# Attention and mixture-of-experts kernel on one core: a decay table made by running products, and another order of loads and transposes at the first expert

## Chip, cores and metric

One Trainium2 chip, one of its cores. The metric is device microseconds of one execution; the kernel before has a median of 269.46 us over three runs (268.55 to 269.71). Engines are TensorE (PE; its weight loads are PEld), VectorE (DVE), ScalarE (ACT), GpSimd (POOL) and SyncE (SP), each with its own queue of instructions, in order.

## The reference

Batch 2, 8 heads, 768 positions, head size 64. Attention is linear with a decay `lam[h]` per head, done in blocks; the result, 1536 tokens of 512, goes to 8 experts, one per token.

```python
intra = einsum('bhic,bhjc->bhij', qb, kb) * Dmask        # Dmask[i,j] = lam**(i-j) for i >= j, else 0
out   = einsum('bhij,bhjd->bhid', intra, vb) + einsum('bhid,bhde->bhie', qb * lam_pow, kv_state)
kv_state = lam_block * kv_state + einsum('bhsd,bhse->bhde', kb * rev_pow, vb)
...
expert = argmax(x @ w_gate); h = relu(x[expert] @ w1); y = gate * (h @ w2)     # w1 512x1024, w2 1024x512
```

## The kernel before, in words

**Attention** (`attention`, L245) works on 12 tiles of 128 tokens, one after the other (loop at L621). A tile needs two loads of 512 KB on SP's queue: `load(s, 0)` brings q and k ("qk"), `load(s, 1)` brings k and v ("kv"); four of each are in flight. `score(s)` (L413, PE at L427) makes the products q k, `mask(s)` (L431, DVE at L437) multiplies them by the decay table `dt`, `decay_k(s)` and `decay_q(s)` (POOL, L406 and L395) scale k by `kp` and q by `qp`, `state(s)` (PE L486, DVE L494 or L496) adds k v to the running state, `attend(s)` (PE L453, L460, ACT L465) makes the output, and `turn`, `gate`, `place`, `scatter` transpose it, choose the expert and write the rows into a DRAM buffer `xs`, sorted by expert. Scores run two tiles ahead; everything of a tile on one engine stands in the written order.

**The decay tables** are made ahead of the loop (L265 to L324). `lam_sb` is loaded; DVE doubles powers of lambda into `z8` on 8 partitions (L279 to L284, one row a head: 127 zeros, a one, then powers); PE transposes a piece of it for `kp` (L302, L303); `z8` is written to the DRAM table `zd` (L305) and read back twice as `dt`, each partition at its own offset (L309). In SP's queue the write stands behind `load(0, 1)` and ahead of `load(1, 0)`; the two reads stand ahead of `load(1, 1)` and of all loads of tiles 2 and 3. DVE then doubles powers into `qp` (L317 to L324). `busy(n)` (L287) issues n matmuls on constants, whose result nothing reads. Between `decay_k(0)` and `decay_q(1)` POOL issues four small DMAs of the gate weights `wg` into `iw` (L606). `tokens()` (L373) is seven small POOL operations on token numbers.

**The experts.** Weights come in pieces of 512 KB, 8 per expert, numbered through (piece 8 is the first of expert 1), in a ring of four raw buffers: `load_w(i)` (L97) on SP, `split_hi(i)` (L104) on ACT rounds it, `split_lo(i)` (L112) on DVE takes the rest and frees the raw buffer. Expert 0 is run in two halves of 128 rows, `first` and `second`, objects of `Solo` (L182): `turn` transposes the rows on PE, `up` is one quarter of the first matrix (12 matmuls of 256 columns, after each second one an ACT evacuation at L216), `cross` transposes the hidden values back (PE L221, ACT L223, DVE L224), `down` is a quarter of the second matrix (6 matmuls of 512 columns). `first` begins within attention; `second` is in `ffn` (L745 to L788). `load_rows(e)` (L138) reads an expert's rows from `xs` and must wait for `pad(e, 0)` and `pad(e, 1)` (POOL, indirect writes that clear unused rows, L129). For experts 1 to 7 (loop at L794, 256 rows at once) the rows are transposed on DVE by `shuffle(e, g)` (L719; the first call also makes the token numbers, L170) and split into two parts by `trans(e, g)` (ACT L729, DVE L730), two of four slices of columns each. The matmuls at L806 of expert 1 read the result, slice by slice.

What sets the order is the text itself: it is compiled with a manual schedule, so each engine runs its instructions in the order written, and each waits for what it reads or overwrites.

Of the kernel before, what the change touches and what calls it, by code (L numbers as in the profile page):

```python
# [41 lines left out]
def kernel(  # L42
# [29 lines left out]
    zd = dram.tile([H, 256], F32, name="zd")  # L72
# [42 lines left out]
    def split_w(i):  # L115
        split_hi(i)
        split_lo(i)
# [127 lines left out]
    def attention():  # L245
        with ExitStack() as c2:
# [10 lines left out]
            def load(s, half):  # L257

                if s >= NTILE:
                    return  # L260
                ld[s, half] = ld_p.tile([P, 2 * DM], F32, tag=f"ld{half}", name="qk" if half == 0 else "kv")
                c = slice(2 * DM * half, 2 * DM * half + 2 * DM)
                nc.sync.dma_start(out=ld[s, half], in_=qkv[s // NC, s % NC, :, c])

            lam_sb = ac.tile([P, HP + 1], F32, name="lam_sb")  # L265
            nc.sync.dma_start(out=lam_sb, in_=lam)
# [3 lines left out]
            z8 = p2.tile([P, 256], F32, tag="tmp", name="z8", bufs=1)[0:H]  # L270
            qp = ac.tile([P, HP, P], F32, name="qp")
            warm = ac.tile([P, 3 * P], F16, name="warm")
            make_identity(nc, ident)
            nc.vector.memset(warm, 1.0)
            one = ac.tile([P, 1], F32, name="one")
            nc.scalar.activation(out=one, in_=warm[:, 0:1], func=AF.Exp)
            nc.vector.memset(z8[:, 0:127], 0.0)
            nc.vector.memset(z8[:, 127:128], 1.0)
            nc.vector.tensor_copy(z8[:, 128:129], lam_sb[0:H, HP:HP + 1])  # L279
            n = 1  # L280
            while n < P:
                nc.vector.tensor_scalar(  # L282
                    out=z8[:, 128 + n:min(128 + 2 * n, 256)], in0=z8[:, 128:128 + n],
                    scalar1=z8[:, 127 + n:128 + n], scalar2=None, op0=ALU.mult,  # L284
                )
                n *= 2
# [9 lines left out]
            kp = ac.tile([P, H, 1], F32, name="kp")  # L296
# [3 lines left out]
            kps = lgb[:, 0:H]  # L300
            busy(11)
            nc.tensor.transpose(kps, z8[:, 127:255], ident[0:H, 0:H])  # L302
            nc.scalar.activation(out=kp, in_=kps, func=AF.Copy)  # L303
            busy(4)
            nc.sync.dma_start(out=zd, in_=z8)  # L305
            load(1, 0)
            dt = ac.tile([P, 2, HP, P], F32, name="dt")
            for t in range(2):
                nc.sync.dma_start(  # L309
                    out=dt[:, t],  # L310
                    in_=bass.AP(tensor=zd.tensor, offset=zd.offset + 256 * t, ap=[[1, P], [512, HP], [1, P]]),
                )
            load(1, 1)
            for i in range(2, 4):
                load(i, 0)
                load(i, 1)
            nc.vector.tensor_copy(qp[:, :, 0:1], lam_sb[:, 0:HP, None])  # L317
            n = 1
            while n < P:
                nc.vector.tensor_tensor(  # L320
                    out=qp[:, :, n:2 * n], in0=qp[:, :, 0:n],
                    in1=qp[:, :, n - 1:n].to_broadcast([P, HP, n]), op=ALU.mult,
                )
                n *= 2  # L324
# [279 lines left out]
            for g in range(2):  # L604
                for r in range(2):
                    nc.gpsimd.dma_start(  # L606
                        out=iw[64 * g:64 * g + 64, r::2, P:P + E], in_=wg[64 * r:64 * r + 64, 2 * g:2 * g + 2]
                    )
            decay_q(1)
            for a in range(HP):  # L610
                score(0, a)
            state(0, (0, 1, 2, 3))
            load(4, 0)
# [3 lines left out]
            busy(5, True)  # L617
            tokens()
            mask(0)
# [55 lines left out]
            load_rows(0, 1)  # L675
            pad(1, 0)
            pad(1, 1)
            load_rows(1)
            load_w(10)
# [3 lines left out]
            load_w(11)  # L683
            first.cross(0)
# [11 lines left out]
    def ffn(first):  # L696
        with ExitStack() as c2:
# [62 lines left out]
            split_hi(10)  # L760
            second.up(0)
            split_lo(10)
            load_w(14)
            second.up(1)
# [291 lines left out]
```

## Time and profile before

| | |
|---|---|
| median of 3 runs | 269.46 us (268.55 to 269.71) |
| profiled execution | 267.77 us, of which the span of the core's instructions 266.0 us |
| PE busy | 243.9 us (92%) |
| DVE, ACT, POOL busy | 157.3, 133.3, 82.5 us |
| mean granted PE clock | 0.967 of 2.4 GHz |
| DMA | 58.67 MB, 221 GB/s on the mean |

The profiled execution lies 1.7 us under the median. Busy PE time counts a matmul from its start to its end, and neighbours overlap; where PE is busy without a gap it sets the pace.

### The profile page before, as it was taken

To read this page: it belongs to the slowest core of one execution; us is meant where nothing else is said; L and a number is where in the kernel's file an instruction comes from. 1 tells how busy PE (TensorE), PEld (TensorE's weight loads), DVE (VectorE), ACT (ScalarE), POOL (GpSimd) and SP (SyncE) were. 2 spreads that over 40 slices of the span, in tenths; PEclk is the share of its full clock that TensorE was granted. 3 is DMA by queue.
4 is the path that set the end of the run, shared out by engine and by line. 5 is a ranking of instruction groups with operands and counts; after the bars stand their busy time and mean duration, and the time that the engine had idled before them with its cause. 6 is when DMAs were issued, how large, how long until landed. Compare 5 with 4: busy or idle time off the path is not lost.

```text
span 266.0 us, 5415 instructions
## 1 busy us (share of the span) xinstructions
PE 243.9 (92%) x2072; PEld 216.4 (81%) x2072; DVE 157.3 (59%) x336; ACT 133.3 (50%) x240; POOL 82.5 (31%) x102
## 2 busy tenths in 40 slices
PE   7679999998899697999999999999999999999960
PEld 3468888877798686988998998998898899899850
DVE  6234576988865267686479268478556937922100
ACT  2023547676674446665466466556545746622110
POOL 4943547998575301001400500410230020020030
PEclk9957999999999889999999999999999999999996
DMA  6997689995756963977498769869839798310010
GB/s 183 247 387 299 201 243 391 391 390 156 223 207 162 356 231 108 268 280 255 166 286 248 265 145 323 249 159 296 262 146 277 265 276 222 117 71 2 1 60 3
DMA packets 27390, 58.67 MB, mean 221 GB/s; under 512 B 5841, under 2 KB 14043, under 8 KB 27360
## 3 DMA queue, kind: packets, MB, share of 16 engines
q1 hardware_dynamic: 23696, 50.89, 60.3%
q0 software_dynamic: 3664, 7.38, 7.4%
q8 instruction: 18, 0.29, 0.5%
q14 instruction: 12, 0.10, 0.1%
HBM read 50.89 MB, written 11.57 MB: 235 GB/s over the span
## 4 chain that ended last, share of the span: by engine, by line
issue 58%; POOL 13%; PE 10%; DMA 8%; DVE 5%; ACT 2%; SPq 1%; POOLq 1%; DVEq 0%
POOL xs L129 6%; POOL out L176 4%; DMA qk<-in_qkv 3%; DMA wraw<-in_wp 3%; PE x L453 2%; PE sc L427 2%; PE tp L509 2%; DVE wlo L112 2%; PE st L486 1%; PE x L460 1%; DMA zd<-z 1%; POOL kd L406 1%; POOL out L869 1%; DMA lam_sb<-in_lam 1%; DVE z L282 1%
## 5 line engine op out<-in xcount | busy, mean ns | idle before, releaser
L112 DVE TENSOR_TENSOR wlo<-wraw,whi 128x1024 fp32r<-128x1024 f32 x64 | 77.3, 1216 | 16.6 <-ACT whi L104 16.6
L104 ACT ACTIVATE whi<-wraw 128x1024 fp32r<-128x1024 f32 x64 | 66.5, 1051 | 10.1 <-DMA wraw<-in_wp 10.1
L806 PE MATMUL h<-xh,whi 128*128 128x256 f32 x224 | 62.2, 278 | 1.5 <-ACT xh L729 1.5
L806 PE MATMUL h<-xl,whi 128*128 128x256 f32 x224 | 62.1, 277 | 0.3 <-DVE xl L730 0.3
L806 PE MATMUL h<-xh,wlo 128*128 128x256 f32 x224 | 62.0, 277 | 0.0
L176 POOL DMA_INDIRECT out<-y,ti x13 | 12.6, 973 | 124.6 <-ACT y L839 124.6
L814 DVE SCALAR_TENSOR_TENSOR hl<-h,hh 128x512 fp32r<-128x512 f32 x28 | 19.4, 692 | 42.2 <-ACT hh L813 42.2
L806 PEld LDWEIGHTS h<-xh,whi 128*128 128x128 f32 x224 | 42.0, 188 | 2.0 <-ACT xh L729 1.7
L806 PEld LDWEIGHTS h<-xl,whi 128*128 128x128 f32 x224 | 42.2, 188 | 0.8 <-DVE xl L730 0.5
L806 PEld LDWEIGHTS h<-xh,wlo 128*128 128x128 f32 x224 | 42.1, 188 | 0.0
L831 PE MATMUL y<-whi,hl 128*128 128x512 f32 x104 | 41.0, 394 | 0.0
L831 PE MATMUL y<-wlo,hh 128*128 128x512 f32 x104 | 40.9, 393 | 0.0
L831 PE MATMUL y<-whi,hh 128*128 128x512 f32 x104 | 40.5, 390 | 0.0
L813 ACT ACTIVATE hh<-h 128x512 fp32r<-128x512 f32 x28 | 16.8, 598 | 40.9 <-PE h L806 40.9
L831 PEld LDWEIGHTS y<-wlo,hh 128*128 128x128 f32 x104 | 19.5, 188 | 4.3
L831 PEld LDWEIGHTS y<-whi,hh 128*128 128x128 f32 x104 | 19.5, 188 | 4.1
L831 PEld LDWEIGHTS y<-whi,hl 128*128 128x128 f32 x104 | 19.6, 188 | 4.0
L437 DVE TENSOR_TENSOR pt<-sc,dt 128x512 f32<-128x512 f32 (+1 forms) x26 | 15.6, 643 | 7.5 <-PE sc L427 4.2
L465 ACT ACTIVATE xT<-x 128x512 f32<-128x512 f32 x12 | 7.1, 593 | 25.5 <-PE x L460 15.6
L129 POOL DMA_INDIRECT xs<-zero,padi x16 | 18.1, 1132 | 4.9 <-issue 4.3
L453 PE MATMUL x<-pt,kv 128*64 128x128 f32 x192 | 15.4, 300 | 1.9 <-DVE pt L437 1.9
L597 POOL DMA_INDIRECT xs<-xg,slot x12 | 16.0, 1333 | 3.7 <-ACT ex L543 1.2
(137 smaller groups left out, 361.2 us busy)
## 6 DMA issues: line engine op xcount, KB each, us to landing
wraw<-in_wp SPq DMA_DIRECT2D x64, 512.0 KB, 4.8
qk<-in_qkv SPq DMA_DIRECT2D x12, 512.0 KB, 7.8
kv<-in_qkv SPq DMA_DIRECT2D x12, 512.0 KB, 8.0
rw<-xs SPq DMA_DIRECT2D x28, 128.0 KB, 3.0
rw<-xs SPq DMA_DIRECT2D x2, 257.0 KB, 2.8
dt<-zd SPq DMA_DIRECT2D x2, 256.0 KB, 4.6
xs<-zero,padi POOLq DMA_INDIRECT x16, 3.5
out<-y,ti POOLq DMA_INDIRECT x13, 5.0
```

The lines of the kernel that those rows point to most:

```text
L104: nc.scalar.activation(out=hi, in_=raw[i], func=AF.Copy)
L112: nc.vector.tensor_tensor(out=lo, in0=t, in1=hi.bitcast(F32), op=ALU.subtract)
L129: i = nc.gpsimd.indirect_dma_start(out=xs, out_offset=bass.IndirectOffsetOnAxis(ap=padi[:, e, t:t + 1], axis=0), in_=zero, in_offset=None, ...
L176: i = nc.gpsimd.indirect_dma_start(out=out, out_offset=bass.IndirectOffsetOnAxis(ap=ti[e][:, t:t + 1], axis=0), in_=y, in_offset=None, bou ...
L437: nc.vector.tensor_tensor(out=pt[s][:, r, a], in0=sc[s][r][:, a], in1=dt[:, r, a], op=ALU.mult)
L453: nc.tensor.matmul(part(h), lhsT=v[:, h], rhs=pt[s][:, h % 2, h // 2], start=(h % 4 < 2), stop=True, skip_group_check=True,)
L465: nc.scalar.activation(out=xT[s], in_=x[:, :, 0:2 * P], func=AF.Copy)
L597: i = nc.gpsimd.indirect_dma_start(out=xs, out_offset=bass.IndirectOffsetOnAxis(ap=slot[:, s:s + 1], axis=0), in_=xg_all[:, s], in_offset= ...
L806: nc.tensor.matmul(ps[:, f], lhsT=a[:, k, fs], rhs=b[:, k], start=(n == 0), stop=(n == 3 * KD - 1),)
L813: nc.scalar.activation(out=hh, in_=ps, func=AF.Relu)
L814: nc.vector.scalar_tensor_tensor(out=hl, in0=ps, scalar=0.0, in1=hh.bitcast(F32), op0=ALU.max, op1=ALU.subtract)
L831: nc.tensor.matmul(yp[t], lhsT=a[:, f, tsl], rhs=b[:, f], start=(p == 0 and f == 0 and n == 0), stop=(p == 3 and f == 1 and n == 2),)
```

## The change

Three groups of edits. **(1) The tables.** `zd` and `z8` are gone. Lambda is loaded spread over all partitions (`lamb`); POOL makes `meet`, a matrix with ones on one antidiagonal; eight DVE scans along rows of 128 (multiply by lambda, add `meet`) write `dt` directly; `kp` is copied from its last column on ACT; `qp` is doubled to 32 columns ahead of `mask(0)` and to 128 behind it. All loads of tiles 1 to 3 are asked for at once, and the gate weights on ACT's queue at the start. `busy` goes from 11 and 4 to 14 early, and from 5 to 6 late. `mask(0)` moves ahead of `state(0)`, `decay_q(1)` behind the rest of `qp`, the gate weights' four DMAs away from POOL. **(2)** `load_w(10)` and `load_w(11)` stand ahead of `load_rows(1)`. **(3)** In `second`, both `shuffle(1, ...)` stand behind `up(0)`, `trans(1, 0)` behind `up(3)`, `trans(1, 1)` behind `down(1)`, and the splits of pieces 10 to 13 come later than they did.

```diff
-            lam_sb = ac.tile([P, HP + 1], F32, name="lam_sb")
-            nc.sync.dma_start(out=lam_sb, in_=lam)
+            lamb = ac.tile([P, 2, HP], F32, name="lamb")
+            nc.sync.dma_start(
+                out=lamb,
+                in_=bass.AP(tensor=lam.tensor, offset=lam.offset, ap=[[0, P], [D * (HP + 1), 2], [1, HP]]),
+            )
             load(0, 0)
             load(0, 1)
...
+            for g in range(2):
+                for r in range(2):
+                    nc.scalar.dma_start(
+                        out=iw[64 * g:64 * g + 64, r::2, P:P + E], in_=wg[64 * r:64 * r + 64, 2 * g:2 * g + 2]
+                    )
+            for i in range(1, 4):
+                load(i, 0)
+                load(i, 1)
...
+            nc.gpsimd.memset(meet, 0.0)
+            nc.gpsimd.affine_select(
+                out=meet, in_=meet, pattern=[[1, P]], compare_op=ALU.not_equal, fill=1.0,
+                base=1 - P, channel_multiplier=1,
+            )
...
-            nc.vector.tensor_copy(z8[:, 128:129], lam_sb[0:H, HP:HP + 1])
-            n = 1
-            while n < P:
-                nc.vector.tensor_scalar(
...
+            dt = ac.tile([P, 2, HP, P], F32, name="dt")
+            for a in range(HP):
+                for r in range(2):
+                    nc.vector.tensor_tensor_scan(
+                        out=dt[:, r, a], data0=lamb[:, r, a:a + 1].to_broadcast([P, P]), data1=meet,
+                        initial=0.0, op0=ALU.mult, op1=ALU.add,
+                    )
+
+            kp = ac.tile([P, H, 1], F32, name="kp")
+            nc.scalar.activation(
+                out=kp.rearrange("p (a r) o -> p a r o", r=2),
+                in_=dt[:, :, :, P - 1:P].rearrange("p r a o -> p a r o"), func=AF.Copy,
+            )
...
-            busy(11)
-            nc.tensor.transpose(kps, z8[:, 127:255], ident[0:H, 0:H])
-            nc.scalar.activation(out=kp, in_=kps, func=AF.Copy)
-            busy(4)
-            nc.sync.dma_start(out=zd, in_=z8)
-            load(1, 0)
-            dt = ac.tile([P, 2, HP, P], F32, name="dt")
-            for t in range(2):
-                nc.sync.dma_start(
...
+            busy(14)
+            def powers(n, end):
...
+            powers(1, 32)
...
             decay_k(0)
-            for g in range(2):
...
-            decay_q(1)
             for a in range(HP):
                 score(0, a)
+            load(4, 0)
+            mask(0)
+            busy(6, True)
+            powers(32, P)
+            decay_q(1)
             state(0, (0, 1, 2, 3))
-            load(4, 0)
             for a in range(HP):
                 score(1, a)
             load(5, 0)
-            busy(5, True)
             tokens()
-            mask(0)
             mask(1)
...
             load_rows(0, 1)
+            load_w(10)
             pad(1, 0)
             pad(1, 1)
-            load_rows(1)
-            load_w(10)
             first.up(2)
             split_hi(7)
             split_lo(7)
             load_w(11)
+            load_rows(1)
...
             second.rest()
-            split_hi(10)
             second.up(0)
-            split_lo(10)
-            load_w(14)
+            shuffle(1, 0)
+            shuffle(1, 1)
             second.up(1)
-            split_hi(11)
+            split_w(10)
+            load_w(14)
             second.up(2)
             second.cross(0)
-            split_lo(11)
+            split_w(11)
             load_w(15)
             second.up(3)
+            trans(1, 0)
+            second.down(0)
+            second.cross(1)
             split_w(12)
             load_w(16)
-            second.down(0)
-            second.cross(1)
-            shuffle(1, 0)
             second.down(1)
-            trans(1, 0)
+            trans(1, 1)
             split_w(13)
             load_w(17)
-            shuffle(1, 1)
             second.down(2)
-            trans(1, 1)
```

## Rows read from the trace of the kernel before

**Rows 1.** The page, part 1: busy us, share of the span, instructions.

```profile
PE 243.9 (92%) x2072; PEld 216.4 (81%) x2072; DVE 157.3 (59%) x336; ACT 133.3 (50%) x240; POOL 82.5 (31%) x102
```

**Rows 2.** Busy time by stretch: PE, PEld, DVE, ACT, POOL; then PE clock, DMA share, GB/s.

```profile
90.00:92.00 2.00, 1.01 (x6) 1.01 (x7) 1.23 (x1) 1.66 (x3) 0.00 (x0) 0.82 1.00 401
92.00:94.00 2.00, 2.00 (x12) 2.00 (x10) 1.16 (x2) 0.81 (x2) 0.00 (x0) 0.50 0.95 340
94.00:98.00 4.00, 4.00 (x20) 3.32 (x20) 2.64 (x5) 2.15 (x3) 0.00 (x0) 0.91 0.56 191
...
125.00:147.00 22.00, 22.00 (x146) 19.99 (x145) 14.71 (x17) 12.75 (x16) 3.94 (x5) 1.00 0.80 239
```

**Rows 3.** Timeline of PE, 84 to 106 us: start, us, instruction, [idle before, releaser].

```profile
84.65 0.28 PE L211 MATMUL solo_ps<-whi,solo_xh 128*128 128x256 f32 x1
...
86.01 0.28 PE L211 MATMUL solo_ps<-whi,solo_xh 128*128 128x256 f32 x1
...
90.99 0.87 PE L221 MATMUL solo_ps<-ident,solo_raw 128*128 128x128 f32 x4 [2.10 <-ACT solo_raw L216]
...
102.75 0.38 PE L806 MATMUL h<-xh,whi 128*128 128x256 f32 x1 [1.47 <-ACT xh L729]
103.48 0.38 PE L806 MATMUL h<-xl,whi 128*128 128x256 f32 x1 [0.34 <-DVE xl L730]
```

**Rows 4.** Timeline of ACT, 73 to 112 us.

```profile
89.39 1.06 ACT L104 ACTIVATE whi<-wraw 128x1024 fp32r<-128x1024 f32 x1 [3.85 <-DMA wraw<-in_wp]
90.36 0.58 ACT L216 ACTIVATE solo_raw<-solo_ps 128x512 f32<-128x512 f32 x1
```

**Rows 5.** Timeline of DVE, 73 to 112 us.

```profile
97.84 0.71 DVE L719 STREAM_TRANSPOSE xf<-rw 128x512 f32<-128x512 f32 x1
...
101.33 0.70 DVE L719 STREAM_TRANSPOSE xf<-rw 128x512 f32<-128x512 f32 x1
```

**Rows 6.** Timeline of SP's queue, 73 to 112 us (a merged row holds waits between its issues).

```profile
79.76 0.33 SPq L162 DMA_DIRECT2D rw<-xs  x1
81.80 1.82 SPq L146 DMA_DIRECT2D rw<-xs  x4
...
84.22 22.57 SPq L97 DMA_DIRECT2D wraw<-in_wp  x10
```

**Rows 7.** The tile rw: time from issue to landing of the loads of rows.

```profile
DMA to landing us min/median/max: 2.4/2.9/7.9
```

**Rows 8.** Timeline of all engines, 0 to 26 us: what the first tiles wait for.

```profile
2.65 1.76 DVE L282 TENSOR_SCALAR z<-z 8x1 f32<-8x1 f32 x7
...
4.51 1.85 DVE L320 TENSOR_TENSOR qp<-qp 128x4 f32<-128x4 f32 x7
...
8.16 0.43 SPq L263 DMA_DIRECT2D qk<-in_qkv  x1
...
10.42 1.31 POOL L395 TENSOR_TENSOR qd<-qk,qp 128x512 f32<-128x512 f32 x1
10.49 0.42 DVE L437 TENSOR_TENSOR pt<-sc,dt 128x256 f32<-128x256 f32 x1 [1.44 <-DMA dt<-zd]
...
13.03 0.21 POOL L380 TENSOR_SCALAR xg<-tokf 128x12 f32<-128x12 f32 x1
14.87 1.04 POOL L406 TENSOR_TENSOR kd<-kv,kp 128x512 f32<-128x512 f32 x1 [1.63 <-DMA kv<-in_qkv]
...
16.83 2.08 PE L427 MATMUL sc<-qk 64*128 64x128 f32 x16 [1.91 <-DMA qk<-in_qkv]
...
18.84 1.12 PE L486 MATMUL st<-kv,kd 128*64 128x64 f32 x16
...
23.97 1.16 PE L427 MATMUL sc<-qk 64*128 64x128 f32 x16
```

**Rows 9.** Busy time by stretch at the start, columns as in rows 2.

```profile
7.00:14.00 7.00, 4.69 (x59) 3.47 (x57) 2.39 (x6) 0.00 (x0) 5.88 (x13) 0.91 0.91 248
14.00:20.00 6.00, 4.09 (x43) 3.46 (x41) 1.80 (x4) 1.55 (x5) 3.30 (x3) 0.50 1.02 396
```

More of the change, by code (lines that the diff above doesn't have):

```diff
@@ L70 @@
     dram = ctx.enter_context(tc.tile_pool(name="dram", bufs=1, space=DRAM))
-    zd = dram.tile([H, 256], F32, name="zd")
     xs = dram.tile([E * ROOM, ROW], F32, name="xs")
@@ L269, in attention @@
             iw = ac.tile([P, KD, P + E], F32, name="iw")
-            z8 = p2.tile([P, 256], F32, tag="tmp", name="z8", bufs=1)[0:H]
+            for g in range(2):
[6 more added lines that the diff above has]
+                load(i, 1)
             qp = ac.tile([P, HP, P], F32, name="qp")
             warm = ac.tile([P, 3 * P], F16, name="warm")
+            nc.vector.memset(warm, 1.0)
+            meet = p2.tile([P, P], F32, tag="tmp", name="meet", bufs=1)
+            nc.gpsimd.memset(meet, 0.0)
[3 more added lines that the diff above has]
+            )
             make_identity(nc, ident)
-            nc.vector.memset(warm, 1.0)
             one = ac.tile([P, 1], F32, name="one")
             nc.scalar.activation(out=one, in_=warm[:, 0:1], func=AF.Exp)
-            nc.vector.memset(z8[:, 0:127], 0.0)
-            nc.vector.memset(z8[:, 127:128], 1.0)
-            nc.vector.tensor_copy(z8[:, 128:129], lam_sb[0:H, HP:HP + 1])
-            n = 1
-            while n < P:
-                nc.vector.tensor_scalar(
[L283 to L286, printed above, removed]
+            dt = ac.tile([P, 2, HP, P], F32, name="dt")
[10 more added lines that the diff above has]
+            )
             def busy(n, late=False):
@@ L294, in busy @@
                     nc.tensor.matmul(ps, lhsT=warm[:, 0:P], rhs=warm, start=True, stop=True)
-            kp = ac.tile([P, H, 1], F32, name="kp")
             lgb = ps_1.tile([P, DM], F32, tag="lg", name="lg")
             iota8 = lgb[:, DM - E:DM]
-            kps = lgb[:, 0:H]
-            busy(11)
-            nc.tensor.transpose(kps, z8[:, 127:255], ident[0:H, 0:H])
-            nc.scalar.activation(out=kp, in_=kps, func=AF.Copy)
-            busy(4)
-            nc.sync.dma_start(out=zd, in_=z8)
-            load(1, 0)
-            dt = ac.tile([P, 2, HP, P], F32, name="dt")
-            for t in range(2):
-                nc.sync.dma_start(
[L310 to L324, printed above, removed]
+            busy(14)
+            def powers(n, end):
+                if n == 1:
+                    for r in range(2):
+                        rs = slice(64 * r, 64 * r + 64)
+                        nc.vector.tensor_copy(qp[rs, :, 0:1], lamb[rs, r, :, None])
+                while n < end:
+                    nc.vector.tensor_tensor(
+                        out=qp[:, :, n:2 * n], in0=qp[:, :, 0:n],
+                        in1=qp[:, :, n - 1:n].to_broadcast([P, HP, n]), op=ALU.mult,
+                    )
+                    n *= 2
+            powers(1, 32)
             mem = [ac.tile([P, HP, D], F32, name=f"mem{i}") for i in range(2)]
@@ L603, in attention @@
             decay_k(0)
-            for g in range(2):
[L605 to L608, printed above, removed]
-            decay_q(1)
             for a in range(HP):
                 score(0, a)
+            load(4, 0)
[3 more added lines that the diff above has]
+            decay_q(1)
             state(0, (0, 1, 2, 3))
-            load(4, 0)
             for a in range(HP):
@@ L759, in ffn @@
             second.rest()
-            split_hi(10)
             second.up(0)
-            split_lo(10)
+            shuffle(1, 0)
+            shuffle(1, 1)
+            second.up(1)
+            split_w(10)
             load_w(14)
-            second.up(1)
-            split_hi(11)
             second.up(2)
             second.cross(0)
-            split_lo(11)
+            split_w(11)
             load_w(15)
             second.up(3)
+            trans(1, 0)
+            second.down(0)
+            second.cross(1)
             split_w(12)
             load_w(16)
-            second.down(0)
-            second.cross(1)
-            shuffle(1, 0)
             second.down(1)
-            trans(1, 0)
+            trans(1, 1)
             split_w(13)
             load_w(17)
-            shuffle(1, 1)
             second.down(2)
-            trans(1, 1)
             split_w(14)
```

## The prediction

> **What bounds the kernel now.** I read the page's busy times first, then stretches, then the timelines of the stretches that are not full. PE is busy 92% of the span [rows 1], and in an expert of the loop all of it: 22.00 of 22.00 us at a clock of 1.00 [rows 2]. There DVE (14.71) and ACT (12.75) have time to spare. So nothing done for the other engines shortens experts 1 to 7 themselves; time can be won only where PE waits or runs at half clock ahead of them, and what is won there moves the whole rest forward. The change touches two such places.
>
> **The start.** The tables' chain is late: DVE doubles `z` from 2.65 us, it goes through DRAM, and the first `mask` waits for it until 10.49 [rows 8]. The round trip also holds SP's queue, so the load that the third tile's scores need is issued only at 8.16, and the scores start at 16.83, released by that DMA [rows 8]. PE is busy 4.69 of the 7 us from 7 to 14, and the clock granted from 14 to 20 is 0.50, 1.2 GHz [rows 9]. The scores of tile 3 start at 23.97 [rows 8].
>
> **The first expert.** `second` begins at 84.65; at 90.99 PE has waited 2.10 us for `solo_raw` [rows 3]. That evacuation stood on ACT behind the split of piece 10, which waited for its weights until 89.39 [rows 4], and those were asked for at 84.22, behind the rows of expert 1 in SP's queue [rows 6]. After the wait the clock is 0.50 for 92 to 94 [rows 2]. Then expert 1 has its matmuls of the first slices done and waits 1.47 and 0.34 us for the later ones [rows 3], since the second DVE transpose ran only at 101.33 [rows 5].
>
> **The change, part by part: the start.** Removed: eight steps on `z`, a PE transpose, a DRAM write and two reads. Lambda lands about when it did, as DVE began at 2.65. Then a chain on DVE and POOL sets the pace, and I add it up to the first instruction of tile 1 on PE, `state(1)`, which needs `kd(1)`:
> - eight scans of 128. No row shows a scan. Bounds: 0.21 (half of the 128x256 row's 0.42 [rows 8]) and 0.70 (the transpose of 512 [rows 5]). I take 0.42, the nearest row, twice the elements, because each product waits for the one before: 8 x 0.42 = 3.4 (1.7 to 5.6);
> - the first seven small operations of `qp`, at 1.85/7 = 0.26 each [rows 8]: 1.8;
> - `mask(0)`, four of 0.42: 1.7;
> - the last two doublings of `qp`, at most 0.42 each: 0.8;
> - on POOL `decay_q(1)` 1.31, `tokens()` from 11.73, where `qd` ends, to 13.24, so 1.5, and `decay_k(1)` 1.04 [rows 8]: 3.9.
>
> 2.65 + 3.4 + 1.8 + 1.7 + 0.8 + 3.9 = 14.2, against 18.84 before [rows 8]: 4.6 earlier. `tokens()` was hidden under a wait for a load (`kd` at 14.87 had waited 1.63 for it [rows 8]) and is now on the path; so is the wait of `decay_q(1)`, behind which both stand on POOL. Moved at nothing: the removed POOL issues of `wg`, the earlier `load(4, 0)`, the one more `busy`, the POOL work for `meet`, which lambda's landing covers (without that cover, a few tenths).
>
> The Trainium skill (DVE: opcode table, instruction layouts, handler registers and perf-mode slots, section "Datapath and trigger behaviour") says that the built-in scan runs at half throughput; with the 0.96 GHz of VectorE in its Trainium Kernel Development and Optimization, "NeuronCore Architecture", that is an estimate of 0.27 us a scan and a sum 1.2 us shorter. No run here shows it yet.
>
> From `state(1)` to the scores of tile 3 took 23.97 - 18.84 = 5.1 us at 0.50. At the full clock it lies between half of that, 2.6, and 5.1. I take 3.7: PE has work nearly throughout, but an evacuation stands in it. That the clock stays up is likely, since `busy`, two tiles' scores, one state and one `attend` now stand close together ahead of 14 us, where PE had been idle 2.3 of 7 us [rows 9]. Gain at the start: 4.6 + 1.4 = **6.0** (2.4 with slow scans and half clock, 8.8 with fast ones and everything at the full clock). The loop behind it is paced by its own engines, and moves forward as a whole.
>
> **The first expert.** Piece 10 is asked for right behind `load_rows(0, 1)`, at 80.1 instead of 84.22 [rows 6], piece 11 with it. It took 89.39 - 84.22 = 5.2 us to land; so 85.3, before ACT needs it. `load_rows(1)` still goes out at 81.80, when its pads have landed: two issues of a few tenths fit into the gap ahead of it. The issues last until 83.62 [rows 6], and a load of rows lands after 2.9 (2.4 to 7.9) [rows 7]: 86.5. DVE then has the two transposes, 1.4 [rows 5], until 88. One `up` takes 86.01 - 84.65 = 1.36 [rows 3], so ACT evacuates at 87.4, unhindered (0.58), and splits piece 10 (1.06) by 89.0 [rows 4]; DVE takes its low part by 90.1 if that lasts as ACT's split does, then the low part of the hidden values, 512 columns as the transpose, 0.7, by 90.8. PE has finished `up` at 84.65 + 4 x 1.36 = 90.1, turned the hidden values, and needs this for its third `down` matmul at about 91. The cover is thin, tenths of a us. Both `trans` end before the last `down`.
>
> What goes: the wait of 2.10; the half clock, as 0.18 x 1.01 + 0.50 x 2.00 + 0.09 x 4.00 = 1.5 [rows 2]; the wait and half-empty stretch at expert 1, 1.47 + 0.34 and the few tenths around one lone matmul between 102.75 and 103.48, together 2.3 [rows 3]. Sum **5.9**. Late next would be piece 14, asked for once piece 10 is split, at 90.1: at 5.2 us it lands at 95.3, and expert 1 needs it only in its second half.
>
> **Sum.** The profiled execution took 267.77, a span of 266.0 and 1.77 around it. 267.77 - 6.0 - 5.9 = 255.9; the median lies 1.7 above that execution, so 257.6, and I say **257.5**.
>
> **The rivals.**
> - *A, forecast:* 254.8 to 260, chance 0.60.
> - *B, a slow chain:* scans at 0.70, or the clock falls all the same in the wait ahead of `state(1)`, some 1 us, which the chain still leaves. Each alone takes back 1.4 to 2.2 us, both 3.6: 259 to 261. For it: the clock fell at the same place before [rows 9]. Chance 0.13.
> - *C, small packets first:* `wg`'s four DMAs of short pieces now share the engines with the first loads. From 7 to 14, when they and the table's reads ran, DMA moved 248 GB/s at 0.91, later 396 at 1.02 [rows 9]: 248 against 353, so 30% of 6.4 busy us, 1.9, went to small packets. The first loads may land up to that later; then `mask(0)` is late by 1 to 1.9 us: 258.5 to 259.5. The Trainium skill (Trainium Kernel Development and Optimization, "Key Constraints") says that DMAs of all queues run on the same 16 engines and interleave, so ACT's queue would give them no room of their own; the trace here has no two such queues at once. Chance 0.07.
> - *D, rows late:* the transposes now stand on DVE ahead of the low parts of piece 10 and of the hidden values. Rows that land at 83.62 + 7.9 = 91.5 [rows 7] end the transposes at 93, and PE waits some 4 us where it waited 2.10, with the half clock behind it: all 5.9 is given back, 263.4. For it: two weights of 512 KB are now in front. Chance 0.11.
> - *E, not the tables:* the loads themselves hold the first tiles, and the start gains nothing: 263.5. For it, DMA is full from 14 to 20 [rows 9]; against it, the load that counted was issued at 8.16, behind the tables. Chance 0.03; with D, no change, 0.03.
> - *F, slower:* the scan itself. From 2.1 us each on (0.42 + (6.0 + 5.9 + 1.35)/8) the DVE chain eats both gains and 0.5%; at 2.5 us it gives 257.5 + 8 x 2.08 = 274. For it: no row shows a scan, and it is serial. Against: 16 ns an element is ten times the 0.42/256 of the row. Chance 0.03.
>
> **Numbers.** 0.5% is 1.35 us, about what a measurement of this kernel can tell from no change. Faster 0.60 + 0.13 + 0.07 + 0.11 + 0.03 = 0.94, same 0.03, slower 0.03. The range takes in A with its bounds, B and C, and those cases of D where the rows are late by a part of it: 254.0 to 262.5.
>
> **What would show it.** Eight scans near 0.42 that end by 6 to 6.5 us; `state(1)` near 14 and scores of tile 3 near 18 us; a clock of 1.00 from 14 to 20 (0.50 means B); the first `kv` not later than before (else C). At the first expert: ACT's evacuation right behind `up(1)` with no wait for weights, no idle PE between `second` and expert 1, the clock at 1.00. A DVE wait for `rw` in front of the transposes of more than 4 us means D. It is wrong as a whole if expert 1 starts less than 8 us earlier than before, or if PE has gaps in experts 1 to 7, which it had not.

## The result, and the profile after

The kernel after takes 259.12 us at the median of four executions (257.75 to 263.02), the kernel before 269.58 beside it (268.55 to 271.29); the ratio is 0.959, 95% interval 0.952 to 0.966. (Some executions of any kernel take some per cent longer, and the ratios leave these out; of the experiment p1_start three of four were such, the profiled one among them, so it has none.) So it is faster, by 10.5 us between these medians. That lies in the range of 254.0 to 262.5, and the forecast of 257.5 was 1.6 too low. The profiled execution took 257.75 us, a span of 256.0, against 267.77 before: 10.0 us less, where the working of the prediction had 11.9.

The page of the kernel after: busy us, share of the span, instructions; then the PE clock granted in 40 equal slices.

```profile
PE 237.9 (93%) x2071; PEld 211.2 (83%) x2071; DVE 158.0 (62%) x335; ACT 132.9 (52%) x240; POOL 81.1 (32%) x100
...
PEclk9999999999999999999999999999999999999995
```

Against [rows 1] PE is busy 6.0 us less with the same work but for one transpose, and the mean granted clock is 0.987 where it was 0.967. The other engines' busy time hardly moved. No slice up to the last one is under 9.

The start of the kernel after, timeline of all engines (start, us, instruction, [idle before, releaser]), answering to [rows 8]:

```profile
3.70 2.77 DVE L297 TENSOR_TENSOR_SCAN dt<-lamb,meet 128x128 f32<-128x128 f32 x8 [2.36 <-DMA lamb<-in_lam]
...
6.52 1.46 PE L438 MATMUL sc<-qk 64*128 64x128 f32 x16 [0.47 <-DMA qk<-in_qkv]
...
8.01 1.42 DVE L448 TENSOR_TENSOR pt<-sc,dt 128x256 f32<-128x256 f32 x4
8.05 1.04 POOL L417 TENSOR_TENSOR kd<-kv,kp 128x512 f32<-128x512 f32 x1 [4.02 <-DMA kv<-in_qkv]
...
10.16 1.27 POOL L406 TENSOR_TENSOR qd<-qk,qp 128x512 f32<-128x512 f32 x1 [1.07 <-DVE qp L329]
...
13.04 1.04 POOL L417 TENSOR_TENSOR kd<-kv,kp 128x512 f32<-128x512 f32 x1
...
14.13 0.69 PE L497 MATMUL st<-kv,kd 128*64 128x64 f32 x16 [1.02 <-POOL kd L417]
...
17.40 1.16 PE L438 MATMUL sc<-qk 64*128 64x128 f32 x16
```

Eight scans in 2.77 us, then the powers and the first mask on DVE, then three steps on POOL (`qd`, the token numbers in the gap, `kd`), and PE takes up `state(1)` at 14.13, where it took it up at 18.84. The scores of tile 3 start at 17.40 instead of 23.97, 6.57 us earlier. The first mask starts at 8.01, just as the scores of tile 0 end (6.52 + 1.46 = 7.98), and these had waited for their load. So by these rows tables and loads are level here, and shorter tables alone would bring the first mask forward by next to nothing.

Busy time by stretch in the kernel after, columns as in [rows 2], answering to [rows 9]:

```profile
7.00:14.00 7.00, 6.03 (x86) 4.68 (x84) 5.30 (x16) 1.54 (x5) 4.45 (x10) 1.00 1.03 408
14.00:20.00 6.00, 5.87 (x104) 5.13 (x104) 3.16 (x12) 2.57 (x10) 4.59 (x5) 1.00 1.02 404
```

The clock from 14 to 20 us is 1.00 where it was 0.50, and PE ahead of it is busy 6.03 of 7 us instead of 4.69. DMA moves 408 GB/s from 7 us on, where it had moved 248 with the reads of the table and the gate weights among the loads (which of the two held it back was not tried).

The first expert in the kernel after, timelines of PE, ACT, DVE and SP's queue in order of time, answering to [rows 3 to 6]:

```profile
77.21 1.81 SPq L145 DMA_DIRECT2D rw<-xs  x4
...
78.12 0.63 PE L192 MATMUL solo_ps<-ident,rw 128*128 128x128 f32 x4 [0.24 <-DMA rw<-xs]
...
79.08 0.54 SPq L150 DMA_DIRECT2D wt<-xs  x1
...
79.98 0.28 PE L210 MATMUL solo_ps<-whi,solo_xh 128*128 128x256 f32 x1
...
83.40 1.05 ACT L103 ACTIVATE whi<-wraw 128x1024 fp32r<-128x1024 f32 x1
...
84.07 0.60 PE L220 MATMUL solo_ps<-ident,solo_raw 128*128 128x128 f32 x4
...
84.61 0.17 DVE L169 TENSOR_SCALAR ti<-wt 128x2 int32<-128x2 f32 x1 [4.39 <-issue]
...
84.79 1.30 DVE L726 STREAM_TRANSPOSE xf<-rw 128x512 f32<-128x512 f32 x2
...
86.02 1.18 DVE L111 TENSOR_TENSOR wlo<-wraw,whi 128x1024 fp32r<-128x1024 f32 x1
...
87.12 0.68 DVE L223 TENSOR_TENSOR solo_hl<-solo_ps,solo_hh 128x512 fp32r<-128x512 f32 x1
...
87.86 0.50 PE L234 MATMUL solo_ps<-whi,solo_hl 128*128 128x512 f32 x1 [0.97 <-DVE solo_hl L223]
...
93.47 0.28 PE L811 MATMUL h<-xh,whi 128*128 128x256 f32 x1
...
104.37 0.39 PE L836 MATMUL y<-whi,hh 128*128 128x512 f32 x1
```

Piece 10 is split at 83.40 without a wait, and PE turns the hidden values at 84.07 without one: the 2.10 of [rows 3] are gone. Expert 1 starts at 93.47, and no PE row from there to 104.37 has a wait in front. What is left is one wait of 0.97 at 87.86 for the low part of the hidden values (`solo_hl`), which DVE makes late: it stood 4.39 us for the rows of expert 1 (put down to "issue"; the next execution's trace names the load, below), then did two transposes and the low part of piece 10 first.

To compare traces I use four marks on PE's path: the scores of tile 3; the first `up` of `second`; the first matmul of expert 1's second half (line 836 above, after every gap at expert 1); and the last store to the output. For the kernel before, the start of expert 1 and the third mark are these rows of its PE timeline:

```profile
100.43 0.28 PE L806 MATMUL h<-xh,whi 128*128 128x256 f32 x1
...
114.07 0.40 PE L831 MATMUL y<-whi,hh 128*128 128x512 f32 x1
```

The last store in the chain of waits of the kernel before, then of the kernel after:

```profile
257.84 0.70 POOL out L869
```

```profile
247.94 0.70 POOL out L874
```

| us | tile 3 | second | second half of expert 1 | last store | span |
|---|---|---|---|---|---|
| before | 23.97 | 84.65 | 114.07 | 257.84 | 266.0 |
| after | 17.40 | 79.98 | 104.37 | 247.94 | 256.0 |
| gain | 6.57 | 4.67 | 9.70 | 9.90 | 10.0 |

So the start gained 6.57, of which 4.67 reached `second`; the first expert gained another 9.70 - 4.67 = 5.03; the rest 0.2. Expert 1's first matmul comes 100.43 - 93.47 = 7.0 us earlier, and the gap behind its first matmuls, which is gone, makes up the other 2.7.

This is one pair of traces, and the trace of before has the latest start of four. On the mean of four traces with the old start (before and three experiments below) and four with the new one (after, after_again, turn_first, lo_behind), tile 3 gains 5.6 us (22.78 to 17.20) and `second` 4.2 (83.99 to 79.82).

### The profile page after: what moved, and what is told of

Its sections match the earlier page's. It is cut to its first block, busy times and chain, and to the rows that moved or that the text cites. A ratio compares the mean times of both kernels' runs of the same rounds, so it can differ in the third digit from the quotient of the medians.

```text
span 256.0 us, 5405 instructions
## 1 busy us (share of the span) xinstructions
PE 237.9 (93%) x2071; PEld 211.2 (83%) x2071; DVE 158.0 (62%) x335; ACT 132.9 (52%) x240; POOL 81.1 (32%) x100
## 4 chain that ended last, share of the span: by engine, by line
issue 58%; POOL 15%; PE 10%; DMA 6%; DVE 6%; ACT 1%; POOLq 1%; SPq 0%; DVEq 0%
POOL xs L128 7%; POOL out L175 5%; DMA wraw<-in_wp 4%; PE sc L438 2%; DVE wlo L111 2%; DMA qk<-in_qkv 2%; PE x L464 2%; PE tp L520 2%; PE st L497 1%; PE x L471 1%; DVE pt L448 1%; POOL qd L406 1%; POOL kd L417 1%; POOL out L874 1%; PE solo_ps L210 1%
## 5 line engine op out<-in xcount | busy, mean ns | idle before, releaser
L175 POOL DMA_INDIRECT out<-y,ti x13 | 13.3, 1025 | 123.7 <-ACT y L844 123.4
L844 ACT ACTIVATE y<-y,wt 128x512 f32<-128x512 f32 x13 | 8.9, 687 | 13.2 <-PE y L836 12.5
```

What stands on the lines that cost most here:

```text
L175: i = nc.gpsimd.indirect_dma_start(out=out, out_offset=bass.IndirectOffsetOnAxis(ap=ti[e][:, t:t + 1], axis=0), in_=y, in_offset=None, bou ...
L844: nc.scalar.activation(out=y, in_=yp[t], func=AF.Copy, scale=wt[e][:, t, 0:1])
```

## The experiments

Twelve kernels, each beside runs of the kernel before on the same chip. Since medians of different chips differ (before: 270.82, 267.46 and 267.05 in the three groups), the reading goes by the marks. Each kernel has one trace: with the same start, `second` lies anywhere from 78.18 to 81.03 in those four, so a us or two at a mark prices nothing by itself. The stretch behind `second` is steadier (24.39 and 24.46 in the two traces of the kernel after).

| us | tile 3 | second | second to second half of expert 1 | last store | span | median | ratio to before, 95% |
|---|---|---|---|---|---|---|---|
| before | 23.97 | 84.65 | 29.42 | 257.84 | 266.0 | 269.58 | |
| after | 17.40 | 79.98 | 24.39 | 247.94 | 256.0 | 259.12 | 0.959 (0.952 to 0.966) |
| p1_start | 18.08 | 78.79 | 31.86 | 254.42 | 262.5 | 264.50 | |
| p2_loads | 23.24 | 84.25 | 27.16 | 254.98 | 263.1 | 265.79 | 0.984 (0.980 to 0.988) |
| p3_turns | 22.20 | 83.05 | 26.75 | 253.36 | 261.5 | 265.40 | 0.983 (0.978 to 0.988) |
| p23_expert | 21.72 | 83.99 | 23.76 | 251.31 | 261.4 | 264.05 | 0.978 (0.971 to 0.986) |
| after_again | 17.12 | 80.08 | 24.46 | 248.10 | 256.4 | 259.11 | 0.974 (0.957 to 0.991) |
| tok_early | 16.23 | 77.25 | 25.76 | 246.57 | 254.7 | 259.50 | 0.978 (0.966 to 0.990) |
| wg_late | 17.26 | 80.19 | 25.95 | 252.44 | 261.9 | 260.29 | 0.976 (0.962 to 0.990) |
| turn_first | 17.11 | 78.18 | 27.29 | 249.03 | 257.1 | 257.97 | 0.969 (0.957 to 0.980) |
| lo_behind | 17.15 | 81.03 | 23.66 | 248.26 | 258.2 | 259.26 | 0.966 (0.958 to 0.975) |
| all_three | 16.31 | 78.60 | 23.67 | 245.84 | 255.8 | 258.68 | 0.970 (0.959 to 0.981) |
| scan_twice | 21.96 | 85.29 | 24.00 | 252.85 | 262.8 | 264.23 | 0.987 (0.977 to 0.996) |
| no_busy | 18.84 | 81.96 | 24.35 | 249.88 | 257.9 | 260.66 | 0.974 (0.961 to 0.987) |

### The parts alone

**p1_start**: group 1 alone; the loads and the order in `second` are those of before. Against the kernel after:

```diff
             load_rows(0, 1)
-            load_w(10)
             pad(1, 0)
             pad(1, 1)
+            load_rows(1)
+            load_w(10)
...
             second.rest()
+            split_hi(10)
             second.up(0)
-            shuffle(1, 0)
-            shuffle(1, 1)
+            split_lo(10)
...
```

> Group 1 of the edits alone (tables, early loads, early order); loads and transposes of the first expert as before. Theory (two separate gains that add up): the scores of tile 3 start near 17.4 us as with the whole change, some 1.9 of the 6.6 us gained there is given back by the end of the first half of expert 0, and the wait for piece 10 with the half clock stays, so about 4.7 us faster than before, near 265. Rival (the first expert's weights are a matter of absolute time, so an earlier start only waits longer for piece 10): under 2 us faster, above 267.5.

Four executions: 264.42 (profiled), 259.81, 264.58, 265.51. The PE and ACT timelines of the first:

```profile
78.79 0.28 PE L210 MATMUL solo_ps<-whi,solo_xh 128*128 128x256 f32 x1
...
85.07 1.06 ACT L103 ACTIVATE whi<-wraw 128x1024 fp32r<-128x1024 f32 x1 [5.39 <-DMA wraw<-in_wp]
...
86.67 1.12 PE L220 MATMUL solo_ps<-ident,solo_raw 128*128 128x128 f32 x4 [3.63 <-ACT solo_raw L215]
...
99.34 0.38 PE L813 MATMUL h<-xh,whi 128*128 128x256 f32 x1 [1.42 <-ACT xh L736]
```

`second` starts 5.86 us earlier than before, but the wait at `cross` is 3.63 where it was 2.10: piece 10 came 4.3 us earlier (89.39 - 85.07), not 5.86. The gap at expert 1 (1.42) is that of [rows 3]. At the last store 257.84 - 254.42 = 3.4 us are left. In this execution the faster start alone runs into a longer wait for weights. The one of 259.81 left no trace and is as short as the kernel after; so how much groups 2 and 3 add to the new start stays open, and what they gain on the old one is read from the next three.

**p2_loads** is group 2 alone, the first diff below, against the kernel before; **p3_turns** is group 3 alone, the second; **p23_expert** is both, with the start of before.

```diff
             load_rows(0, 1)
+            load_w(10)
             pad(1, 0)
             pad(1, 1)
-            load_rows(1)
-            load_w(10)
...
             load_w(11)
+            load_rows(1)
```

```diff
-            split_hi(10)
             second.up(0)
-            split_lo(10)
-            load_w(14)
+            shuffle(1, 0)
+            shuffle(1, 1)
             second.up(1)
-            split_hi(11)
+            split_w(10)
+            load_w(14)
...
```

> Groups 2 and 3 alone on the kernel before (order of loads, and earlier transposes). Theory: no half clock after 90 us, no gap at expert 1, some 5.3 us faster, near 264.3; scores of tile 3 at 24 us as before. Rival (the late rows hold DVE, as in case D): PE waits more than 4 us for the low part of the hidden values, under 2 us faster.

> Group 2 alone: pieces 10 and 11 asked for ahead of the rows of expert 1, transposes where they were. Theory: the wait of 2.1 us for the evacuation behind the split of piece 10 and the half clock behind it go (3.6 us), the gap at expert 1 (2.3 us) stays: near 266. Rival (the weights only swap places with the rows, which come late instead): within 1 us of before.

> Group 3 alone: transposes earlier and splits later, loads in the old order. Theory: the evacuation no longer stands behind the split of piece 10, but the low part of the hidden values stands behind the low part of piece 10, which lands near 89.4: PE waits some 1.5 to 2 us there, has no gap at expert 1; some 3.5 to 4 us faster, near 265.8. Rival (the order of loads is what matters): within 1 us of before.

Timeline of p23_expert:

```profile
83.99 0.28 PE L211 MATMUL solo_ps<-whi,solo_xh 128*128 128x256 f32 x1
...
87.99 0.17 DVE L170 TENSOR_SCALAR ti<-wt 128x2 int32<-128x2 f32 x1 [3.76 <-DMA wt<-xs]
...
91.23 0.50 PE L235 MATMUL solo_ps<-whi,solo_hl 128*128 128x512 f32 x1 [0.68 <-DVE solo_hl L224]
```

Timelines of p2_loads (its gap at expert 1), and of p3_turns (its rows and its wait at `second`); behind each, the clock that followed (PE busy; clock, DMA share, GB/s):

```profile
98.97 0.38 PE L806 MATMUL h<-xh,whi 128*128 128x256 f32 x1 [1.57 <-ACT xh L729]
...
100.00:102.00 2.00, 2.00 (x11) 0.50 0.12 47
```

```profile
85.90 0.17 DVE L170 TENSOR_SCALAR ti<-wt 128x2 int32<-128x2 f32 x1 [2.62 <-DMA wt<-xs]
...
88.73 1.06 ACT L104 ACTIVATE whi<-wraw 128x1024 fp32r<-128x1024 f32 x1 [2.17 <-DMA wraw<-in_wp]
...
90.33 0.50 PE L235 MATMUL solo_ps<-whi,solo_hh 128*128 128x512 f32 x1 [1.18 <-ACT solo_hh L223]
...
92.00:96.00 4.00, 4.00 (x14) 0.58 0.94 254
```

From `second` to the second half of expert 1, the loads alone gain 29.42 - 27.16 = 2.3, the order alone 2.7, both 5.7. Each leaves what the other takes: with the loads alone the wait of 2.10 is gone and the gap at expert 1 stays (1.57); with the order alone expert 1 has no gap, and piece 10 is late (88.73). Both fell short of what was expected (3.6, and 3.5 to 4), as the half clock did not go: with the loads alone it moved behind the gap at expert 1 (0.50 from 100 to 102 us), with the order alone it stayed behind the waits for the hidden values (0.58 from 92 to 96). With both it is gone (1.00 from 84 to 104 us). The start of before varied by up to 2.25 us among these traces (tile 3 at 21.72 to 23.97), so their last stores do not price groups 2 and 3; the stretch does.

### The start in detail

**after_again** is the kernel after once more, as a yardstick for the next three. **tok_early** calls `tokens()` ahead of `decay_k(0)`, off the path of `decay_k(1)`. **wg_late** asks for the gate weights behind the copy of `kp` on ACT, so that they no longer share the DMA engines with lambda. The two diffs, against the kernel after:

```diff
+            tokens()
             decay_k(0)
...
-            tokens()
             mask(1)
```

```diff
-            for g in range(2):
-                for r in range(2):
-                    nc.scalar.dma_start(
...
             nc.scalar.activation(
                 out=kp.rearrange("p (a r) o -> p a r o", r=2),
                 in_=dt[:, :, :, P - 1:P].rearrange("p r a o -> p a r o"), func=AF.Copy,
             )
+            for g in range(2):
+                for r in range(2):
+                    nc.scalar.dma_start(
...
```

> The changed kernel itself, as the control of the runs beside it: 257.8 to 259.5 us, PE's clock at 1.00 from 14 to 20 us.

> The changed kernel with tokens() put ahead of decay_k(0) on POOL, where POOL waits for k and v anyway. Theory (the seven token operations stand on the path from the tables to the first state of tile 1): state(1) starts near 13.1 instead of 14.1 us, PE's wait of 1.0 there goes, the whole is 1 us faster. Rival (the loop gives it back, since weights and loads come when they come): 1 us earlier at tile 3, but within 0.4 us of the control at the end.

> The changed kernel with the four loads of the gate weights moved on ACT's queue from the very start to behind the copy of kp. Theory (case C in part: their short pieces make lambda land at 3.7 us instead of 2.5, and four loads on SP wait for them): scans start near 2.6 us, state(1) about 1 us earlier, k and v of tile 0 land near 6.8, about 1 us faster. Rival (lambda's own load, 256 pieces instead of 128, is what takes longer): scans still start near 3.7, no change.

after_again repeats the marks within 0.3 us, and its DVE row names the load: 4.45 us for `wt`, the token weights, which travel behind the rows. In tok_early the scores of tile 3 come at 16.23, about 0.9 earlier, as `state(1)` no longer waits for `kd`, and `second` at 77.25. But its rows wait:

```profile
83.25 0.17 DVE L169 TENSOR_SCALAR ti<-wt 128x2 int32<-128x2 f32 x1 [5.75 <-DMA wt<-xs]
```

```profile
86.49 0.51 PE L234 MATMUL solo_ps<-whi,solo_hl 128*128 128x512 f32 x1 [2.67 <-DVE solo_hl L223]
```

These two rows are of its DVE and PE timelines. `second` started 2.7 us ahead of the kernel after, PE then waited 2.67 instead of 0.97, and the last store came 1.4 earlier; the median, 259.50 against 259.11 of after_again, shows none of the 1 us expected. wg_late starts its scans at 3.54 instead of 3.57 in after_again: lambda's lateness does not come from the gate weights, and nothing is gained at the start (its later marks are those of its slowest execution, 263.69, and are not read).

**turn_first** takes the transposes ahead of the token numbers, to see which load DVE stands for (in `shuffle` of the kernel after):

```diff
                 if g == 0:
-                    tokens_of(e)
...
+                if g == 1:
+                    tokens_of(e)
```

> The changed kernel with the token numbers of an expert made behind its two DVE transposes instead of ahead of them. Theory (the load of weights and token numbers per row, the last of the five issues, is what DVE waits for near 84.6 us, while the rows are there earlier): the transposes start 1 us or more earlier, PE's wait of 0.97 for the low part of the hidden values goes, 1 us faster. Rival (the rows themselves land at that time): transposes start within 0.3 us of the control, no change.

Its DVE timeline:

```profile
84.24 1.30 DVE L725 STREAM_TRANSPOSE xf<-rw 128x512 f32<-128x512 f32 x2 [5.82 <-DMA rw<-xs]
```

Here it is the rows themselves, `rw`, that DVE stands for. The transposes start 0.5 to 0.7 us earlier than in the two traces of the kernel after, between the theory's 1 and its rival's 0.3, although `second` had started 1.8 us earlier. PE then waited 2.63 for `solo_hl`, and the clock of 80 to 92 us fell to 0.86. A wait of that length does not settle the clock: behind the 2.67 of tok_early it stayed at 1.00. The median of turn_first, 257.97, lies 1.1 under after_again, but the two intervals overlap over most of their length, and its trace is no faster.

### The wait that is left

**lo_behind** has the low part of piece 10 behind that of the hidden values on DVE. **all_three** has that, the early token numbers of tok_early, and piece 11 asked for behind the rows of expert 1. Against the kernel after, lo_behind and then what all_three adds at the loads:

```diff
-            split_w(10)
-            load_w(14)
+            split_hi(10)
             second.up(2)
             second.cross(0)
+            split_lo(10)
+            load_w(14)
```

```diff
-            load_w(11)
             load_rows(1)
+            load_w(11)
```

> The kernel after, with the low part of piece 10 moved on DVE behind the low part of the hidden values. Theory (rows of expert 1 land late, and DVE, in order, makes the transposes, then 1.3 us of low part of piece 10, before the low part that PE waits for): PE's wait for solo_hl falls by 1.0 to 1.3 us, from 0.97 (257.75 us) and 1.42 (259.11 us) to 0.3 or less; expert 1 starts about 1 us earlier; about 257.5 median. Rival (the rows' landing alone holds the end; the low part of piece 10 is wanted just behind): the wait goes over to the next matmul, which takes the low part of piece 10, with under 0.4 us gained; 258.5 to 259.5.

> The kernel after, with three moves: token numbers ahead of decay_k(0), the low part of piece 10 behind that of the hidden values, and piece 11 asked for behind the rows of expert 1 instead of ahead of them. Theory (one 512 KB weight fewer in front brings the rows to DVE about 1.3 us sooner, so that the 0.9 us that the earlier token numbers win at the start is no longer waited away): scores of tile 3 near 16.2, no PE wait above 0.4 us between second and expert 1; 256 to 257.5 median. Rival (the rows land when the whole stretch of transfers allows it, whatever stands in front, or piece 11 is now late): the transposes still wait over 4 us, 258.5 to 260.

In lo_behind no PE row between `second` and expert 1 has a wait, and the stretch is 23.66, which is 0.73 less than in the kernel after. But its `second` started at 81.03, a us later, as PE had waited 1.76 for the rows of the second half (0.24 in the kernel after, 1.66 in after_again), and the median, 259.26, is no better. all_three, three rows of its PE and DVE timelines:

```profile
16.31 1.16 PE L438 MATMUL sc<-qk 64*128 64x128 f32 x16
...
81.95 0.17 DVE L169 TENSOR_SCALAR ti<-wt 128x2 int32<-128x2 f32 x1 [3.11 <-DMA wt<-xs]
...
102.27 0.39 PE L837 MATMUL y<-whi,hh 128*128 128x512 f32 x1
```

The rows were there at 81.95 instead of 84.61, and expert 1's second half 2.1 us earlier than in the kernel after, as was the last store (245.84). Weights in front delay the rows: from the end of the issue of `wt` to DVE's use it is 81.95 - 78.26 = 3.7 us here, with piece 10 alone in front, and 84.61 - 79.62 = 5.0 in the kernel after, with pieces 10 and 11; in p3_turns, with neither, 85.90 - 82.88 = 3.0. With both in front it is 4.9 to 6.6 in all nine traces; the 3.7 and the 3.0 have one trace each. Yet the span is 255.8, 0.2 less than the kernel after's, for a reason behind the last store (below). The median, 258.68, lies 0.6 under lo_behind's, the ratio (0.970) does not lie under it (0.966), and its interval overlaps that of the kernel after. So it is ahead of the kernel after by the marks of one trace; the times do not show it.

### The chain, and the clock

**scan_twice** makes each of the eight scans twice. **no_busy** leaves out `busy(14)` and `busy(6, True)`, matmuls whose result nothing reads. Against the kernel after:

```diff
-            for a in range(HP):
+            for a in [*range(HP), *range(HP)]:
```

```diff
-            busy(14)
...
-            busy(6, True)
```

> The kernel after, with each of the eight scans made twice: 8 x 0.346 = 2.77 us more on DVE ahead of everything else of the start; the output is the same. Theory (the chain of scans, powers, masks and POOL sets the start): state(1) goes from 14.13 to 16.5 to 17, the scores of tile 3 from 17.40 to 19.5 to 20.2; some of it is then saved at the wait for expert 1's rows (0.97 to 1.42 us of PE's wait), so the end is 1.2 to 2.5 us later: 260.2 to 261.5. Rival (PE's own work or the loads set the start): state(1) under 15.2 and the end under 0.8 us later, 259.1 to 259.9.

> The kernel after, without busy(14) and busy(6, True), the idle matmuls that keep TensorE occupied ahead of the first tiles; nothing of the output depends on them. Theory (the clock of 1.00 from 14 to 20 us rests on them): the granted clock falls to 0.50 within the first 20 us, the scores of tile 3 come 1 to 2.5 us later than 17.40, the end 0.5 to 2 us later: 259.6 to 261. Rival (the denser order of the first tiles holds the clock by itself): clock at 1.00 from 14 to 20, scores of tile 3 within 0.4 of 17.40, the end unchanged: 258.5 to 259.5.

DVE and PE timelines of scan_twice, and its clock by stretch (PE busy; clock, DMA share, GB/s):

```profile
3.73 5.25 DVE L297 TENSOR_TENSOR_SCAN dt<-lamb,meet 128x128 f32<-128x128 f32 x16 [2.39 <-DMA lamb<-in_lam]
...
17.16 0.73 PE L497 MATMUL st<-kv,kd 128*64 128x64 f32 x16 [2.80 <-POOL kd L417]
...
21.96 1.16 PE L438 MATMUL sc<-qk 64*128 64x128 f32 x16
```

```profile
18.00:20.00 2.00, 2.00 (x24) 0.50 0.80 297
```

The scans took 5.25 us for 2.77 and the small steps behind them 0.75 more, and `state(1)` came 3.0 us later (17.16 for 14.13): the chain is the path. PE's longer wait (2.80 for 1.02) was followed by half clock, 0.50 from 18 to 20 us, and `state(1)` to tile 3 took 4.80 instead of 3.27. The last store is 4.9 us later, the median 5.1 above after_again: twice what I had expected, since I had left the clock out. PE timeline of no_busy, and its clock:

```profile
6.75 2.08 PE L437 MATMUL sc<-qk 64*128 64x128 f32 x16 [6.75 <-DMA qk<-in_qkv]
...
14.38 1.26 PE L437 MATMUL sc<-qk 64*128 64x128 f32 x16
```

```profile
7.00:10.00 3.00, 2.47 (x28) 1.00 1.03 404
```

Tile 0's scores take 2.08, as in [rows 8] at a clock of 0.50, where the kernel after has its own in 1.46 and tile 1's in 1.16. Tile 3's scores come 1.44 later, the last store 1.9, the median 1.5 above after_again. I had expected the clock record to fall, and it did not: it reads 1.00 all the way, so here the durations tell the half speed and the record does not. The idle matmuls do not secure the full speed either: in p1_start, which has them, tile 0's scores took 2.08 too, at a record of 1.00. DVE then waited for them, and tile 3 came at 18.08:

```profile
8.69 1.42 DVE L448 TENSOR_TENSOR pt<-sc,dt 128x256 f32<-128x256 f32 x4 [1.01 <-PE sc L438]
```

The Trainium skill (TensorE: Matmul & The Clock Gate, section "Seeing it yourself") warns that clock events of a trace can be unreliable; these rows of no_busy and p1_start agree.

## Why the prediction was right, and where it was short

**The chain at the start** was right to 0.1 us (14.13 for 14.2), through errors that cancel. The step "lambda lands about when it did" failed: DVE waited for it until 3.70, not 2.65, 1.05 late. (Little was lost by it, as tile 0's scores ended only at 7.98, a wait that the sum has at nothing.) The scans were 0.35 each, for 0.42 taken: 2.77 for 3.4. The Trainium skill's half throughput (DVE: opcode table, instruction layouts, handler registers and perf-mode slots, "Datapath and trigger behaviour") had given an estimate of 0.27: the trace lies between. The small operations and the mask were 0.6 cheaper together (10.16 - 6.47 = 3.7 for 4.3); POOL's three steps took 14.08 - 10.16 = 3.9, as summed. That `tokens()` came onto the path was right: tok_early takes 0.9 of it off.

**The clock** held, and from `state(1)` to tile 3 it took 3.27 for 3.7. Gain at tile 3: 6.57 for 6.0, and 5.6 on the mean of four traces each. Rival B's mechanism is real: in scan_twice the slow chain does bring the half clock with it, so its two halves come together rather than each alone. no_busy, in one trace, prices `busy` at some 1.5 us of it.

**"The loop behind it is paced by its own engines, and moves forward as a whole"** is the step that failed most: 1.9 of the 6.57 were gone at `second`, and 1.4 of 5.6 on the mean of four traces each. From tile 3 to `second` it took 60.68 before and 62.58 after. In the fourteen traces this stretch lasts 60.7 to 61.1 in six and 62.3 to 63.9 in eight, and the difference is PE's waits in it, 2.8 to 3.3 us in sum in the first six, 4.2 to 5.7 in the others: for the rows of the second half (up to 1.76), and ahead of states, mostly at 27 to 33 and at 44 to 53 us. In the kernel after it is above all the state at 46.30. Its row with two of ACT and DVE ahead of it:

```profile
43.19 1.06 ACT L103 ACTIVATE whi<-wraw 128x1024 fp32r<-128x1024 f32 x1 [2.26 <-DMA wraw<-in_wp]
...
45.88 0.17 DVE L547 TENSOR_TENSOR oh<-lg,i 128x8 f16<-128x8 f32 x1 [1.16 <-ACT xg L532]
...
46.30 0.69 PE L497 MATMUL st<-kv,kd 128*64 128x64 f32 x16 [1.14 <-issue]
```

The split of a piece stood 2.26 us for its weights on ACT, the copy `xg` behind it came late, DVE waited 1.16 for that, and PE 1.14 in turn (by the order of the rows; no run took this wait away). p1_start and turn_first, with the same start, lost next to nothing on the way (60.71 and 61.07), and p23_expert, with the old start, took 62.27. So this is no fixed price of the change. What makes one execution late there is not settled.

**The first expert**: 5.9 forecast; 5.7 by p23_expert alone, 5.0 in the kernel after, 5.75 in lo_behind (29.42 - 23.66). The wait for piece 10, the half clock and the gap at expert 1 all went, as said. The mis-sized term is "a load of rows lands after 2.9": it took 5.0 from the last issue, and 5.6 from 79.02, the end of the four issues that the prediction counts (it left out the one of `wt` behind them). That is rival D in part, with two weights in front as it said and at 5.0, not its 7.9. The "thin cover" was thinner than that, and PE waited 0.97 to 1.42 for `solo_hl` in the two traces of the kernel after, which the low part of piece 10 delayed on DVE.

**Two of the prediction's own signs of being wrong came true.** DVE waited 4.39 for the rows, and "more than 4 us means D"; yet PE waited 0.97 and not some 4, since DVE's wait counts from 80.2, some 7 us ahead of PE's need. And expert 1 starts 7.0 us earlier, where less than 8 was to mean "wrong as a whole": 9.6 was forecast there (6.0, 2.10 and 1.5), and of the 2.6 missing 1.3 lie ahead of `second` and 1.3 between `second` and expert 1. The gap at expert 1 then gave 2.7 for 2.3. So the range held with two of its steps short, as it was wide enough for them.

**The other rivals.** C: the first `kd` was at 8.05, later than before (6.80 in the trace of before), but the mask on DVE began at 8.01 and does not need it, and POOL itself then waited 1.07 for `qp`; no loss by the time of `state(1)`, and wg_late gains nothing there. (That the trace of before "has no two such queues at once" is not so: POOL's four issues of the gate weights, from 7.78 to 10.43, ran beside SP's loads.) E and F: the tables did hold the start, though after the change the loads are level with them, and a scan is at 0.35, far from 2.1.

**Sum.** 4.67 + 5.03 + 0.2 = 9.9 against 11.9: 1.3 short at the start's way to `second`, 0.9 short at the first expert, 0.2 won in expert 1 and behind.

## What to carry to other kernels

A gain at one stage is worth what the next load in order lets through: measure it at marks along the path, because the later waits (weights for ACT, rows for DVE) can swallow it, as here 1.9 of 6.57 in one pair of traces, and undo the parts singly to see which. When a load is moved ahead, count how long those now behind it take to land, and put the work that waits for them behind whatever TensorE needs first on the same engine. A chain ahead of the first matmuls can cost more than its own length: in scan_twice `state(1)` came 3.0 us later, and tile 3, at half clock for part of the way, 4.6.

## What was not expected of the hardware

**The end of the span.** From the end of the last store's row to the end of the span it is 266.0 - 258.54 = 7.5 us in the kernel before, 256.0 - 248.64 = 7.4 in the kernel after, and 7.3 to 7.6 in nine of the fourteen traces; 9.2 to 9.4 in four (p23_expert, lo_behind, all_three, scan_twice) and 8.8 in wg_late. The timeline has no row there. So 1.9 us of a difference between two executions can lie behind all the work. What decides it was not tried.

**Lambda's load.** Spread over all partitions (256 pieces of 16 B) it took 2.6 us from issue to landing in wg_late and 2.7 in after_again, where the one of before, 128 pieces of 20 B, took 1.6. The Trainium skill (DMA: Bandwidth & Descriptors, "Why small descriptors are slow (HBM only)") names a fixed cost for each piece, which these runs agree with but do not separate from other causes, such as the loads of tiles 0 and 1 issued right behind it.

**Loads on SP that wait for another queue.** In the waits of the kernel after, four loads of q, k and v on SP stood, as the profile puts it, behind gate-weight DMAs that ACT had issued (us in all, times, longest):

```profile
SPq L262 <- DMA iw<-in_wg: 4.7, 4, 2.1
```

With the gate weights moved (wg_late) SP waited 7.5 us (4.4 + 3.1) for earlier loads of its own instead, and the scores of tile 3 came at 17.26 against 17.12: it did not matter here.
